# Turning the gathered tokens of five experts: from TensorE to VectorE, by way of DRAM

## The chip, the core and the metric

The program runs on one core of a Trainium2 chip. A core has five engines that run their own queues of instructions and wait for one another by semaphores: TensorE (PE, matrix products; its weight loads are shown as PEld), VectorE (DVE), ScalarE (ACT), GpSimd (POOL) and SyncE (SP, which here issues most DMAs). SBUF and PSUM are memories of 128 partitions; PE writes to PSUM alone. The metric is device time in microseconds of one execution, the median of several runs.

## The reference

Three layers follow one another on B x S = 2304 tokens of 512 values: attention that keeps the 32 largest scores of each row, a gated layer, and a layer with eight experts of which each token uses one. The change is in the third:

```python
def _moe2_ref(x, expert_emb, tau, w1, w2):
    xn = x / (np.linalg.norm(x, axis=-1, keepdims=True) + 1e-06)
    en = expert_emb / (np.linalg.norm(expert_emb, axis=-1, keepdims=True) + 1e-06)
    logits = xn @ en.T / tau
    expert_idx = np.argmax(logits, axis=1)
    ...
    for e in range(E):
        mask = expert_idx == e
        ...
        h = np.maximum(x[mask] @ w1[e], 0.0)
        out[mask] = gate_w[mask, None] * (h @ w2[e])
```

## The kernel before, in words

Attention and most of the gated layer fill the first 768 us, ordered by lists of names that are written out by hand. They leave the gated layer's result in DRAM (`y_dram`, one row of 512 values for each token), and a table in DRAM (`tbl`) that lists the tokens of each expert. What follows is the expert layer, again with an order written by hand (`tc.manual_schedule()`): each engine runs its instructions in the order of the code.

The experts are sorted by their number of tokens. Rank r has room for `CAPS[r]` tokens, (480, 352, 320, 304, 256, 256, 256, 240), cut into blocks of 128: 4 + 3 + 3 + 3 + 2 + 2 + 2 + 2 = 21 blocks. "Expert r" below is the expert of rank r. The order of work is `TURNS` = 0, 1, 2, 3, 4, 6, 7, 5; the main loop (line 1225) goes over r, with `then`, the next expert, and `nn`, the one after it.

All products are made of three: a number is split into a high part (rounded to the fp32r format) and the low rest, and high x high, low x high and high x low are added. For one expert r the loop does this:

- **The f loop** (lines 1229 to 1240). For each of eight blocks of 128 hidden columns, `first` (line 961) makes 12 products on PE (line 953, into a PSUM tile of the pool "ph", which has two buffers); ACT writes `hh`, the high part of the clipped result (line 958), and DVE `hl`, the low part (line 959).
- Between the blocks, work for the next expert is put in. `turn_in` (line 1036), after blocks 2, 4 and 6, takes one block of 128 gathered tokens (`xg`), which has a token on each partition, and turns it so that the features are on the partitions: four PE transposes of 128x128 into a PSUM tile `pxt` of the pool "px" (line 1044, two buffers), then ACT writes the high part `xh_` (line 1045) and DVE the low part `xl_` (line 1046). `split_2`, after the odd blocks, splits a quarter of the next expert's second weights: ACT writes `h` (line 860), DVE `l` (line 861).
- Experts 2 and 3 (`ACROSS`) make their second product transposed, and it is turned back in the next expert's f loop by `turn_out` (line 1003) after blocks 0, 2 and 4, with four PE transposes into `pxo`, in the same pool "px"; `leave` then sends the rows to the output with a DMA on POOL (line 1027) and starts the gather of a gate (line 1013).
- **After the f loop** SP issues the four loads of the second weights of `nn` (`load2`, line 857), which wait until the split of `then`'s second weights has read their buffer, and POOL the gathers of `nn`'s tokens (`get`, line 1033) from `y_dram`.
- Then the second product (`second`, line 987, or `columns`, line 1000). After its first block the four pieces of `then`'s first weights are split (`split_1`), and SP issues the loads of `nn`'s first weights (`load1`, line 848).

The features of a token are numbered on the partitions by blocks of 128: partition p of slice k holds feature 128k + p, as `w1r` (line 777) and the slices `xg[:, 128k : 128k+128]` in `turn_in` have it. Elsewhere in the kernel there is another form: `route`, in the gated layer, writes a tile to `yq_dram` and loads it back in another order, so that a transpose of 32x32 squares on DVE (line 685) completes the turn; partition p of slice k then holds feature 4p + k. The last two tiles of that layer are turned by PE with slices of step four (line 1166).

Of the kernel before, what the change touches and what calls it, by code (L numbers as in the profile page):

```python
# [8 lines left out]
F32 = mybir.dt.float32  # L9
# [20 lines left out]

TURNS = (0, 1, 2, 3, 4, 6, 7, 5)
ACROSS = (2, 3)
TURNED = 12
NEG = -3.0e38
BIG = 2.0 ** 100
# [25 lines left out]
def fused_kernel(tc: tile.TileContext, *args):  # L61

    nc = tc.nc
    y_dram = tc.dram_tile([NT + 1, DM], F32, name="y_dram")
    g_dram = tc.dram_tile([NT + 128, 1], F32, name="g_dram")
    tbl = tc.dram_tile([E * STRIDE, 2], I32, name="tbl")

    yq_dram = tc.dram_tile([8, 128, 128], F32, name="yq_dram")  # L70
    lo_dram = [tc.dram_tile([8, 128, 1024], F32, name=f"lo_dram{n}") for n in range(2)]
    with ExitStack() as held:
        pools = [held.enter_context(tc.tile_pool(name=n, bufs=b, **kw)) for n, b, kw in
                 (("const", 1, {}), ("sm", 4, {}), ("fs", 1, {}), ("ps_a", 1, {"space": PSUM}))]
        flag = pools[0].tile([1, 2], I32, name="flag")
        consts = {}
        over_ = layers(tc, *args, y_dram, yq_dram, g_dram, tbl, lo_dram, flag, pools, consts)
        rare = nc.values_load(flag[0:1, 1:2], min_val=0, max_val=NT + 1)  # L78
        with tc.If(rare > 0):
            over_()  # L80
            again = nc.values_load(flag[0:1, 0:1], min_val=0, max_val=1)
            with tc.If(again > 0):
                layers(tc, *args, y_dram, yq_dram, g_dram, tbl, lo_dram, None, pools, consts)()


class Held:
# [7 lines left out]
        return self.tiles[name]  # L94


def layers(tc: tile.TileContext, qt, kt, v, w_in, w_out, embt, tau, w1, w2, out, y_dram, yq_dram, g_dram, tbl, lo_dram, flag, pools, consts):
    nc = tc.nc
    exact = flag is None

# [3 lines left out]
    ident, ent = both[:, 4 * E:], both[:, :4 * E].rearrange("p (k e) -> p k e", k=4)  # L104
# [33 lines left out]
    def bank():  # L138
        turn[1] ^= 1
        return bank_t[turn[1]]  # L140
# [66 lines left out]
    for q in range(8):  # L207
        c = slice(256 * q, 256 * q + 256)
# [368 lines left out]
    moe = deque()  # L577
# [196 lines left out]
    late = {}  # L774
    mb = ExitStack()
    evs, idts, tok, ws1 = {}, {}, {}, {}
    w1r = w1.rearrange("e (k p) f -> p e k f", p=128)

    def blocks(r):
        return [(o // 128, o, min(128, CAPS[r] - o)) for o in range(0, CAPS[r], 128)]  # L780
# [63 lines left out]
    def load1(r, parts=range(4)):  # L844
        if 0 in parts:
            ws1[r] = raw1[r] = late["w1" if r == 0 else "wb"].tile([128, 4, F2], F32, tag="raw", name="a1")
        for k in parts:
            nc.sync.dma_start(out=raw1[r][:, k, :], in_=w1r[:, bass.ds(evs[r], 1), k, :].rearrange("p o f -> p (o f)"))
# [4 lines left out]
    def load2(r, parts=range(4)):  # L853
        if 0 in parts:
            ws2[r] = raw2[r] = late["w1"].tile([128, 8, DM], F32, tag="raw", name="a2")
        for k in parts:
            nc.sync.dma_start(out=raw2[r][:, 2 * k:2 * k + 2, :], in_=w2r[:, bass.ds(evs[r], 1), 2 * k:2 * k + 2, :].rearrange("p o k d -> p (o k) d"))
# [67 lines left out]
    if True:  # L925
# [15 lines left out]
        hs, xg_, gg_, xt_ = {}, {}, {}, {}  # L941
# [19 lines left out]
        def first(r, f, c0, c1):  # L961
            hidden(r, f, c0, c1)
            hidden_out(r, f, c0, c1)
# [66 lines left out]
        def get(r, b):  # L1030
            n, o, m = b
            xg_[r, n] = xg = late["xg"].tile([128, DM], F32, tag="xg", name="xg")
            nc.gpsimd.indirect_dma_start(out=xg[:m, :], out_offset=None, in_=y_dram,
                                         in_offset=bass.IndirectOffsetOnAxis(ap=idts[r][:m, n, 0:1], axis=0))

        def turn_in(r, b):
            n, o, m = b
            if r not in tok:
                tok[r] = [(tk if TURNS.index(r) % 2 else late["tk"]).tile([128, 4, CAPS[TURNS.index(r) % 2]], F32R, tag=t, name=t) for t in ("xh_", "xl_")]
            xh_, xl_ = tok[r]  # L1040
            xg = xg_.pop((r, n))
            pp = bank().rearrange("p (k n) -> p k n", k=4) if moe else px.tile([128, 4, 128], F32, tag="px", name="pxt")
            for k in range(4):
                nc.tensor.transpose(pp[:, k, :m], xg[:m, 128 * k:128 * k + 128], ident[:m, :m])
            nc.scalar.copy(xh_[:, :, o:o + m], pp[:, :, :m])
            nc.vector.tensor_tensor(xl_[:, :, o:o + m], pp[:, :, :m], xh_[:, :, o:o + m].bitcast(F32), op=ALU.subtract)

# [41 lines left out]
        bl = {r: blocks(r) for r in range(E)}  # L1089
# [43 lines left out]
        with tc.manual_schedule():  # L1133
            at.close()
            pools_()
            for n in range(len(moe)):
                a = moe[0]
# [18 lines left out]
            px = mb.enter_context(tc.tile_pool(name="px", bufs=2, space=PSUM))  # L1156
# [57 lines left out]
            todo = [(r, b) for r in TURNS for b in bl[r]]  # L1214
# [10 lines left out]
            for r, then, nn in zip(TURNS, TURNS[1:] + (None,), TURNS[2:] + (None, None)):  # L1225
                c0 = 256 if r == 0 else 0
                b2 = bl[r][2:] if r == 0 else bl[r]
                todo = deque(bl[then]) if then is not None else deque()
                for f in range(8):
                    first(r, f, c0, CAPS[r])  # L1230
                    if back and f in (0, 2, 4):
                        turn_out(*back[0])
                        leave(*back.popleft())
                    if todo and f in (2, 4, 6):
                        turn_in(then, todo.popleft())
                    if then is not None and f % 2:
                        split_2(then, f // 2)
                    if r == 0 and f > 5:
                        leave(0, bl[0][f - 6])
                    if r == 1 and f in (0, 3, 6):  # L1240
                        finish_counts(f // 3)
                if nn is not None:
                    load2(nn)
                    for x in bl[nn]:
                        get(nn, x)
                for n, b in enumerate(b2 if r not in ACROSS else range(4)):
                    if r in ACROSS:
                        columns(r, n)
                    elif n == len(b2) - 1 and then is None:
                        last_block(r, b)  # L1250
                    else:
                        second(r, b, range(8))
                    if n == 0 and then is not None:
                        for k in range(4):
                            split_1(then, k)
                        if nn is not None:
                            load1(nn)
                    if r not in ACROSS:
                        leave(r, b)
                if r in ACROSS:  # L1260
                    back.extend((r, b) for b in b2)
                if nn is None and then is not None:
                    nc.gpsimd.drain()  # L1263
# [93 lines left out]
```

## Time and profile before

| | us |
|---|---|
| median of 3 runs | 1019.8 (1019.55 to 1022.65) |
| profiled execution, its own time | 1016.89 |
| its span, first to last instruction | 1015.1 |
| PE busy | 940.5 (93% of the span) |
| DVE busy | 769.4 (76%) |
| ACT busy | 714.1 (70%) |
| POOL busy | 631.7 (62%) |
[...]

The profile is of one execution. In a row of busy time by stretch stand the stretch, its length, then the busy time of PE, PEld, DVE, ACT and POOL with the number of instructions, PE's granted clock, the DMA engines' busy share and GB/s. Busy time of PE is that of overlapping records: products are pipelined, so the time that one costs is the distance from its start to the next start. In the timelines the columns are start, duration, engine, line, operation, what is written and read, and in brackets the idle time of the engine before it with what ended it.

### The profile page before, as it was taken

To read this page: it belongs to the slowest core of one execution; us is meant where nothing else is said; L and a number is where in the kernel's file an instruction comes from. 1 tells how busy PE (TensorE), PEld (TensorE's weight loads), DVE (VectorE), ACT (ScalarE), POOL (GpSimd) and SP (SyncE) were. 2 spreads that over 40 slices of the span, in tenths; PEclk is the share of its full clock that TensorE was granted. 3 is DMA by queue.
4 is the path that set the end of the run, shared out by engine and by line. 5 is a ranking of instruction groups with operands and counts; after the bars stand their busy time and mean duration, and the time that the engine had idled before them with its cause. 6 is when DMAs were issued, how large, how long until landed. Compare 5 with 4: busy or idle time off the path is not lost. (4 is left out here: it accounts for less than half of the span.)

```text
span 1015.1 us, 20760 instructions
## 1 busy us (share of the span) xinstructions
PE 940.5 (93%) x7172; PEld 825.0 (81%) x7172; DVE 769.4 (76%) x2353; ACT 714.1 (70%) x1441; POOL 631.7 (62%) x786
## 2 busy tenths in 40 slices
PE   3666787999999999999999999999999999999997
PEld 1344576889899988998999987889898888999996
DVE  7999999999989989889999898871234464455551
ACT  4899898888789788798787787774335553455551
POOL 4788999877778788688687775674242353034220
PEclk9965799999999999999999999999999999999999
DMA  5555777664456755556565485375585475545620
GB/s 199 180 166 172 236 242 260 216 206 148 141 175 192 238 183 140 153 166 211 195 183 147 141 256 191 123 235 187 170 280 195 134 245 202 185 153 194 235 83 23
DMA packets 93265, 187.25 MB, mean 184 GB/s; under 512 B 15837, under 2 KB 36464, under 8 KB 93151
## 3 DMA queue, kind: packets, MB, share of 16 engines
q1 hardware_dynamic: 88591, 175.97, 54.2%
q0 software_dynamic: 4416, 9.80, 3.0%
q8 instruction: 58, 0.95, 0.4%
q14 instruction: 56, 0.46, 0.1%
q10 hardware_dynamic: 144, 0.07, 0.0%
HBM read 160.56 MB, written 22.03 MB: 180 GB/s over the span
## 5 line engine op out<-in xcount | busy, mean ns | idle before, releaser
L490 POOL TENSOR_TENSOR s<-s,z 128x576 f32<-128x576 f32 x144 | 189.8, 1319 | 62.1 <-ACT z L486 61.6
L605 PE MATMUL bank_h<-xh,vh 128*128 128x256 f32 x576 | 170.8, 297 | 0.0
L605 PE MATMUL bank_h<-xh,lo 128*128 128x256 f32 x576 | 163.2, 283 | 0.7 <-DMA lo<-lo_dram 0.7
L605 PE MATMUL bank_h<-xl,vh 128*128 128x256 f32 x576 | 163.0, 283 | 0.0
L472 DVE MAX8 A<-left 128x8 f32<-128x288 f32 (+1 forms) x288 | 159.4, 594 | 0.0
L523 PE MATMUL bank_t<-both,s 128*128 128x128 f32 x648 | 107.8, 290 | 29.5 <-ACT pt L528 17.3
L523 PEld LDWEIGHTS bank_t<-both,s 128*128 128x128 f32 x648 | 81.3, 148 | 51.7 <-ACT pt L528 22.8
L528 ACT COPY pt<-bank_t 128x384 f32<-128x384 f32 x216 | 101.5, 479 | 26.4 <-PE bank_t L523 26.4
L624 POOL TENSOR_TENSOR gl<-u,gh 128x512 fp32r<-128x512 f32 x72 | 93.2, 1294 | 42.4 <-ACT gh L621 42.3
L444 ACT COPY s<-ps_sc 128x576 f32<-128x576 f32 x143 | 92.3, 645 | 36.0 <-PE ps_sc L433 13.3
L640 PE MATMUL y<-wh,gh 128*128 128x512 f32 x288 | 116.8, 406 | 0.0
L486 ACT ACTIVATE z<-s,nb 128x576 bf16<-128x576 f32 x144 | 112.3, 780 | 4.7 <-POOL nb L480 4.5
L640 PE MATMUL y<-lo,gh 128*128 128x512 f32 x288 | 113.5, 394 | 0.1
L640 PE MATMUL y<-wh,gl 128*128 128x512 f32 x288 | 113.3, 393 | 0.0
L496 ACT ACTIVATE s<-s,nb 128x576 f32<-128x576 f32 x144 | 113.0, 786 | 0.2 <-POOL s L490 0.2
L605 PEld LDWEIGHTS bank_h<-xh,lo 128*128 128x128 f32 x576 | 110.1, 191 | 0.9 <-DMA lo<-lo_dram 0.9
L605 PEld LDWEIGHTS bank_h<-xl,vh 128*128 128x128 f32 x576 | 110.5, 192 | 0.3
L605 PEld LDWEIGHTS bank_h<-xh,vh 128*128 128x128 f32 x576 | 110.4, 192 | 0.3
L1027 POOL DMA_INDIRECT out_dram<-ob,idt x21 | 23.1, 1100 | 135.2 <-ACT ob L1020 108.5
L541 PE MATMUL bank_a<-pt,vt 128*64 128x128 f32 (+1 forms) x1600 | 94.9, 278 | 0.6 <-ACT pt L528 0.6
L959 DVE SCALAR_TENSOR_TENSOR hl<-ph,hh 128x256 fp32r<-128x256 f32 (+5 forms) x72 | 31.7, 440 | 84.1 <-ACT hh L958 83.7
L861 DVE TENSOR_TENSOR l<-a,h 128x1024 fp32r<-128x1024 f32 x64 | 76.8, 1234 | 24.2 <-ACT h L860 23.6
(263 smaller groups left out, 2636.2 us busy)
## 6 DMA issues: line engine op xcount, KB each, us to landing
lo<-lo_dram SPq DMA_DIRECT2D x144, 512.0 KB, 4.5
a<-in_moe_w_dram SPq DMA_DIRECT2D x64, 512.0 KB, 6.3
vt<-in_v_dram SPq DMA_DIRECT2D x28, 320.0 KB, 5.1
w<-in_moe_w_in_dram SPq DMA_DIRECT2D x16, 512.0 KB, 4.5
w<-in_moe_w_out_dram SPq DMA_DIRECT2D x16, 512.0 KB, 5.5
lo_dram<-wf SPq DMA_DIRECT2D x32, 256.0 KB, 2.4
qraw<-in_q_dram SPq DMA_DIRECT2D x48, 128.0 KB, 3.9
krs<-in_k_dram SPq DMA_DIRECT2D x16, 288.0 KB, 4.2
```

What stands on the lines that cost most here:

```text
L444: nc.scalar.copy(sbuf[i % NS][:, :, HS * g:HS * g + HS], ps_[i][:, :, :HS])
L472: nc.vector.max(A[:, n, 8 * r:8 * r + 8], src[:, n, :w])
L486: nc.scalar.activation(zb_[n], tile_of(i, n), AF.Relu, bias=sel[i][1][:, n, 1:2], scale=-BIG)
L490: nc.gpsimd.tensor_tensor(s, s, zb_[n], op=ALU.subtract)
L496: nc.scalar.activation(s, s, AF.Exp, bias=sel[i][1][:, n, 0:1], scale=SCALE, accum_out=sums[i][:, n:n + 1])
L523: nc.tensor.transpose(pp[:, 128 * k:128 * k + 128], e[:, 128 * (3 * c + k):128 * (3 * c + k) + 128], ident)
L528: nc.scalar.copy(pts[i][:, 3 * c:3 * c + 3, :].rearrange("p k n -> p (k n)"), tb_.pop((i, c))[:, :384])
L541: nc.tensor.matmul(av[64 * n:64 * n + 64, c0:c1], vt[:, k, 64 * n:64 * n + 64], pt[:, k + 5 * n if k < 4 else 4, c0:c1], start=(o == 0), s ...
L605: nc.tensor.matmul(ph[:, a, :], w, x[:, k, :], start=(k == 0 and n == 0), stop=(k == 3 and n == 2))
L624: nc.gpsimd.tensor_tensor(state[q][1], state.pop((q, "u")).rearrange("p (a n) -> p a n", a=2), state[q][0].bitcast(F32), op=ALU.subtract)
L640: nc.tensor.matmul(state["y"][o], x[:, a, c], w, start=(f == 0 and n == 0), stop=(f == 15 and n == 2))
L861: nc.vector.tensor_tensor(lo, x, hi.bitcast(F32), op=ALU.subtract)
```

## The change

Five of the eight experts (`CARRIED` = 3, 4, 5, 6, 7; all but the first three of the order of work) have their tokens turned by DVE in place of PE. As soon as their rows are gathered, SP stores them to a DRAM tile `xq_dram` (`carry_out`), ahead of the loads of the second weights. After the first block of the second product it loads them back in another order (`carry_in`), ahead of the loads of the first weights: partition 32a + c then holds 128 features (those of group a) of tokens 4c to 4c + 3. In the next f loop DVE transposes the 32x32 squares into `pxt` (`turn_x`, after blocks 1, 3 and 5), and `turn_in` goes on from there without its PE transposes. The gathers of these experts always bring 128 rows, since whole tiles are stored. As the result has feature 4p + k on partition p of slice k, the first weights are loaded in that order for all experts, and the PE transposes that stay (experts 0, 1, 2) take slices of step four.

```diff
-    w1r = w1.rearrange("e (k p) f -> p e k f", p=128)
+    w1r = w1.rearrange("e (p k) f -> p e k f", k=4)
...
             xg_[r, n] = xg = late["xg"].tile([128, DM], F32, tag="xg", name="xg")
+            if r in CARRIED:
+                m = 128
...
+        def carry_out(r):
+            for n, o, m in bl[r]:
+                nc.sync.dma_start(out=xq_dram[n].rearrange("a p x -> p a x"), in_=xg_[r, n].rearrange("p (a x) -> p a x", a=4))
+
+        def carry_in(r):
+            for n, o, m in bl[r]:
+                nc.sync.dma_start(out=xg_[r, n], in_=xq_dram[n].rearrange("a (c i) x -> (a c) (i x)", i=4))
+
+        turned_ = {}
+
+        def turn_x(r, b):
+            n, o, m = b
+            turned_[r, n] = pp = px.tile([128, 4, 128], F32, tag="px", name="pxt")
+            nc.vector.transpose(pp.rearrange("p k (c i) -> p i k c", i=4), xg_[r, n].rearrange("p (i r k) -> p i k r", i=4, k=4))
...
-            pp = bank().rearrange("p (k n) -> p k n", k=4) if moe else px.tile([128, 4, 128], F32, tag="px", name="pxt")
-            for k in range(4):
-                nc.tensor.transpose(pp[:, k, :m], xg[:m, 128 * k:128 * k + 128], ident[:m, :m])
+            if r in CARRIED:
+                pp = turned_.pop((r, n))
+            else:
+                pp = bank().rearrange("p (k n) -> p k n", k=4) if moe else px.tile([128, 4, 128], F32, tag="px", name="pxt")
+                for k in range(4):
+                    nc.tensor.transpose(pp[:, k, :m], xg[:m, :].rearrange("p (x k) -> p k x", k=4)[:, k], ident[:m, :m])
...
                     first(r, f, c0, CAPS[r])
+                    if todo and f in (1, 3, 5) and then in CARRIED:
+                        turn_x(then, todo[0])
...
                 if nn is not None:
-                    load2(nn)
                     for x in bl[nn]:
                         get(nn, x)
+                    if nn in CARRIED:
+                        carry_out(nn)
+                    load2(nn)
...
                         if nn is not None:
+                            if nn in CARRIED:
+                                carry_in(nn)
                             load1(nn)
```

How the instructions stand: first DVE in expert 6's f loop, from `hl` of block 1 on. Before (`hl` and `hh` are the parts of the first product of block ph, `a`, `h` and `l` the second weights of expert 7 and their parts, `xh__` and `xl__` its tokens' parts):

```order
1316 L959 SCALAR_TENSOR_TENSOR hl_11812<-ph2_11828,hh_11811 128x256
1317 L861 TENSOR_TENSOR l2_11844<-a2_11723,h2_11843 128x1024
1318 L959 SCALAR_TENSOR_TENSOR hl_11812<-ph2_11847,hh_11811 128x256
1319 L1046 TENSOR_TENSOR xl__11863<-pxt_11864,xh__11862 128x4x128
1320 L959 SCALAR_TENSOR_TENSOR hl_11812<-ph2_11871,hh_11811 128x256
1321 L861 TENSOR_TENSOR l2_11844<-a2_11723,h2_11843 128x1024
1322 L959 SCALAR_TENSOR_TENSOR hl_11812<-ph2_11888,hh_11811 128x256
1323 L1046 TENSOR_TENSOR xl__11863<-pxt_11903,xh__11862 128x4x112
```

The same place of DVE with the change:

```order
1323 L961 SCALAR_TENSOR_TENSOR hl_11810<-ph2_11826,hh_11809 128x256
1324 L1053 STREAM_TRANSPOSE pxt_11841<-xg_11717 128x4x128
1325 L863 TENSOR_TENSOR l2_11844<-a2_11723,h2_11843 128x1024
1326 L961 SCALAR_TENSOR_TENSOR hl_11810<-ph2_11847,hh_11809 128x256
1327 L1068 TENSOR_TENSOR xl__11863<-pxt_11841,xh__11862 128x4x128
1328 L961 SCALAR_TENSOR_TENSOR hl_11810<-ph2_11866,hh_11809 128x256
1329 L1053 STREAM_TRANSPOSE pxt_11881<-xg_11719 128x4x128
1330 L863 TENSOR_TENSOR l2_11844<-a2_11723,h2_11843 128x1024
1331 L961 SCALAR_TENSOR_TENSOR hl_11810<-ph2_11885,hh_11809 128x256
```

A transpose stands between `hl` of each of the blocks 1 and 3 and the split of the second weights behind it. Then SP, around the loads of one expert's second and first weights (rows of register work between the loads are marked ISA). Before:

```order
480 L857 ISA
481 L857 DMA a_11410<-in_moe_w_dram 128x2x512
482 L857 ISA
483 L857 DMA a_11410<-in_moe_w_dram 128x2x512
484 L857 ISA
485 L857 DMA a_11410<-in_moe_w_dram 128x2x512
486 L857 ISA
487 L857 DMA a_11410<-in_moe_w_dram 128x2x512
488 L848 ISA
489 L848 DMA a_11456<-in_moe_w_dram 128x1024
```

The same place of SP with the change:

```order
484 L1042 DMA xq_dram<-xg 128x4x128 x2
485 L859 ISA
486 L859 DMA a_11412<-in_moe_w_dram 128x2x512
487 L859 ISA
488 L859 DMA a_11412<-in_moe_w_dram 128x2x512
489 L859 ISA
490 L859 DMA a_11412<-in_moe_w_dram 128x2x512
491 L859 ISA
492 L859 DMA a_11412<-in_moe_w_dram 128x2x512
493 L1046 DMA xg<-xq_dram 128x512 x2
494 L850 ISA
495 L850 DMA a_11456<-in_moe_w_dram 128x1024
```

The two stores stand ahead of the second weights' loads, the two loads back between them and the first weights' loads.

## Rows read from the trace of the kernel before

**Rows 1.** F loops of experts 2, 3, 4, 6, 7: length, busy time by engine.

```profile
855.66:871.16 15.50, 15.50 (x110) 15.21 (x108) 8.31 (x13) 8.00 (x14) 4.76 (x5) 1.00 0.22 66
885.24:900.87 15.63, 15.63 (x119) 15.60 (x118) 8.11 (x12) 9.22 (x16) 7.36 (x8) 1.00 0.32 113
914.20:927.90 13.70, 13.70 (x118) 13.68 (x118) 7.48 (x12) 8.93 (x16) 6.75 (x7) 1.00 0.38 139
939.05:951.32 12.27, 12.27 (x105) 12.27 (x104) 7.27 (x12) 7.31 (x13) 4.80 (x4) 1.00 0.65 237
962.46:974.22 11.76, 11.76 (x105) 11.73 (x104) 7.06 (x12) 7.28 (x13) 2.45 (x2) 1.00 0.51 204
```

**Rows 2.** Timeline of PE, expert 6: a turn after block 2, and the second product's start.

```profile
943.33 0.60 PE L1044 MATMUL pxt<-both,xg 128*128 128x128 f32 x4
943.69 0.36 PE L953 MATMUL ph<-xh__11614,h 128*128 128x256 f32 x1
943.89 0.28 PE L953 MATMUL ph<-xl__11615,h 128*128 128x256 f32 x1
944.00 0.28 PE L953 MATMUL ph<-xh__11614,l 128*128 128x256 f32 x1
...
951.32 0.39 PE L987 MATMUL po<-h,hh 128*128 128x512 f32 x1
```

**Rows 3.** Timeline of PE: a turn with slices of step four.

```profile
769.79 0.65 PE L1166 MATMUL pxt<-both,ysl 128*128 128x128 f32 x4
770.20 0.36 PE L953 MATMUL ph<-xh__9917,h 128*128 128x256 f32 x1
```

**Rows 4.** Line 685, ns min/median/max of one, first and last start.

```profile
L685 DVE STREAM_TRANSPOSE yt<-ya x12: 1078/1100/1129, 240.4 to 614.2; 128x512 f32<-128x512 f32 x12
```

**Rows 5.** Groups by line on DVE: busy us, mean ns of one, idle before.

```profile
L454 DVE TENSOR_TENSOR left<-ps_sc,s 128x288 f32<-128x288 f32 x72 | 32.9, 457 | 2.5
L453 DVE TENSOR_TENSOR ps_sc<-ps_sc,s 128x288 f32<-128x288 f32 x72 | 32.8, 456 | 12.7 <-ACT s L444 12.2
```

**Rows 6.** Timeline of DVE in expert 6's f loop, blocks 1 and 2.

```profile
942.52 0.42 DVE L959 SCALAR_TENSOR_TENSOR hl<-ph,hh 128x256 fp32r<-128x256 f32 x1 [1.00 <-ACT hh L958]
943.45 1.22 DVE L861 TENSOR_TENSOR l<-a,h 128x1024 fp32r<-128x1024 f32 x1 [0.51 <-ACT h L860]
944.60 0.42 DVE L959 SCALAR_TENSOR_TENSOR hl<-ph,hh 128x256 fp32r<-128x256 f32 x1
944.93 0.68 DVE L1046 TENSOR_TENSOR xl__11863<-pxt,xh__11862 128x512 fp32r<-128x512 f32 x1
```

**Rows 7.** Timeline of DVE in expert 1's f loop.

```profile
833.90 0.50 DVE L959 SCALAR_TENSOR_TENSOR hl<-ph,hh 128x352 fp32r<-128x352 f32 x1
```

**Rows 8.** Timeline of PE at the same place.

```profile
834.46 0.43 PE L953 MATMUL ph<-xh__10431,h 128*128 128x352 f32 x1 [0.44 <-DVE hl L959]
```

**Rows 9.** Timeline of POOL after expert 4's f loop: the last gather.

```profile
928.97 0.94 POOL L1033 DMA_INDIRECT xg<-y_dram,idt  x1 [0.30 <-issue]
```

**Rows 10.** DMA issues from 800 to 1005 us: count, KB, median us to landing.

```profile
a<-in_moe_w_dram SPq DMA_DIRECT2D x48, 512.0 KB, 6.5
...
xg<-y_dram,idt POOLq DMA_INDIRECT x14, 3.4
```

**Rows 11.** Timeline of SP: expert 7's second weights, then its first.

```profile
930.72 2.09 SPq L857 DMA_DIRECT2D a<-in_moe_w_dram  x4
935.26 1.94 SPq L848 DMA_DIRECT2D a<-in_moe_w_dram  x4
```

**Rows 12.** Timeline of ACT in expert 6's f loop: the first split.

```profile
942.38 1.04 ACT L860 CAST h<-a 128x1024 fp32r<-128x1024 f32 x1
```

**Rows 13.** Line 674, the store in pieces of 512 bytes (512 KB).

```profile
L674 SPq DMA_DIRECT2D yq_dram<-ysb x6: 462/466/470, 217.2 to 582.3; - x6
...
DMA to landing us min/median/max: 4.7/4.7/4.8
```

**Rows 14.** Line 678, the load back in pieces of 2 KB (512 KB).

```profile
DMA to landing us min/median/max: 5.2/6.0/6.3
```

More of the change, by code (lines that the diff above doesn't have):

```diff
@@ L32 @@
 ACROSS = (2, 3)
+CARRIED = (3, 4, 5, 6, 7)
 TURNED = 12
@@ L70, in fused_kernel @@
     yq_dram = tc.dram_tile([8, 128, 128], F32, name="yq_dram")
+    xq_dram = tc.dram_tile([3, 4, 128, 128], F32, name="xq_dram")
     lo_dram = [tc.dram_tile([8, 128, 1024], F32, name=f"lo_dram{n}") for n in range(2)]
@@ L76, in fused_kernel @@
         consts = {}
-        over_ = layers(tc, *args, y_dram, yq_dram, g_dram, tbl, lo_dram, flag, pools, consts)
+        over_ = layers(tc, *args, y_dram, yq_dram, g_dram, tbl, xq_dram, lo_dram, flag, pools, consts)
         rare = nc.values_load(flag[0:1, 1:2], min_val=0, max_val=NT + 1)
@@ L82, in fused_kernel @@
             with tc.If(again > 0):
-                layers(tc, *args, y_dram, yq_dram, g_dram, tbl, lo_dram, None, pools, consts)()
+                layers(tc, *args, y_dram, yq_dram, g_dram, tbl, xq_dram, lo_dram, None, pools, consts)()
 class Held:
@@ L94, in tile, with layers @@
         return self.tiles[name]
-def layers(tc: tile.TileContext, qt, kt, v, w_in, w_out, embt, tau, w1, w2, out, y_dram, yq_dram, g_dram, tbl, lo_dram, flag, pools, consts):
+def layers(tc: tile.TileContext, qt, kt, v, w_in, w_out, embt, tau, w1, w2, out, y_dram, yq_dram, g_dram, tbl, xq_dram, lo_dram, flag, pools, consts):
     nc = tc.nc
```

## The prediction

> **What bounds the kernel now.** I read the page first (PE is busy for 93% of the span, and in the last ten slices the other engines are far below that), then the busy time by stage, then PE's own order of time. The change touches only the last stage, the second expert layer, which runs from about 768 us to the end. [rows 1] cuts out the loop over eight column blocks ("the f loop", lines 1229 to 1240) of the five experts during which a changed turn is done: 2, 3, 4, 6 and 7, in the order of work, which turn in the tokens of experts 3, 4, 6, 7 and 5. [...] So PE sets the end here, and every microsecond taken off PE comes off the time, unless another engine holds PE up. That DVE is at half load says less than it seems: PE has two PSUM buffers for the first product (the pool "ph"), so block f+2 can't start before DVE has written `hl` of block f.
>
> **What is removed.** Four PE transposes for each of 11 blocks of tokens (3 blocks for expert 3, two each for 4, 6, 7, 5). What one group costs is its slot on PE, not the 0.27 us of one record, since the records overlap. In [rows 2] the group of expert 7's first block starts at 943.33, the next product at 943.69, and that product's successor 0.20 us later, where 0.11 or 0.12 is usual: 0.36 + 0.08 = 0.44 us. A group that follows a turn_out pays the refill anyway (0.36), and one of 48 rows less. Two whole and one short block (1.1), 2 x 0.36 in each of two loops (1.4), 0.44 + 0.40, and 2 x 0.44: about 4.3 us. That is the most that the change can give.
>
> **What the remaining PE turns pay.** Because the weights' rows are now taken in steps of four, the ten groups of experts 0, 1 and 2 read their tokens with a step of 16 bytes. Such groups exist: line 1166 takes 0.41 us from its start to the next product [rows 3], 0.05 more than [rows 2]. The capacities make 21 blocks; 11 lose their group, 10 keep it: 10 x 0.05 = +0.5 us.
>
> **What DVE gets.** One STREAM_TRANSPOSE of 128x512 for each block, in program order between `hl` of block 1, 3 or 5 and the split of the second weights. The kernel has this instruction already: 1.10 us, 1.08 to 1.13 over 12 runs [rows 4], from SBUF into SBUF, reading with a step of 16 bytes and writing without one. The new one reads with the same step, and writes into PSUM with a step of 16 bytes. That the destination is PSUM costs nothing in the nearest rows: the same 128x288 operation takes 456 ns into PSUM and 457 ns into SBUF [rows 5]. No row has a stepped write of DVE. I take 1.10; the lower bound is 0.69, what DVE takes to stream the same 512 columns out of PSUM [rows 6], the upper 2.2, if each stepped write takes twice as long as a plain one.
>
> [...]
>
> **Where DVE's time lies.** Not beside idle time. I walk expert 6's loop with starts from [rows 6]. There `hl` of block 1 starts at 942.52, the split at 943.45, the next `hl` at 944.60 (1.15 after the split), `xl` at 944.93 (0.33 after), for 0.68. The only gap is the 0.58 us after 942.87, when DVE is free and the split still waits for ACT. After the change: the turn at 942.87, the split 1.03 later at 943.90 (an instruction behind another starts some 0.07 before that one's end), `hl` of block 2 at 945.05, done at 945.47. PE, without its transposes, is through with block 3 at 943.33 + 1.42 ((12.27 - 0.84) / 8 from rows 1) = 944.75 and waits for that `hl`. Expert 1's loop has such a wait: `hl` starts at 833.90 and runs 0.50 us [rows 7], and PE starts at 834.46 [rows 8], 0.06 us after its end, to which I add the 0.08 us of refill from rows 2. So block 4 starts in effect at 945.6, 0.85 us late. `xl` at 945.38, `hl` 3 at 945.98, the second turn at 946.33, the split at 947.36, `hl` 4 from 948.51 to 948.93; block 5 ends at 948.45, and block 6 waits until 949.1. Two more blocks give 951.9, where the trace has 951.32 [rows 2]: **+0.6 us in place of -0.85**.
>
> The others go by the same walk. From `hl` 1 to `hl` 3 a pair of blocks with a turn takes DVE 945.98 - 942.52 = 3.46 us, some 0.1 more where there are more columns. PE's block is the length in [rows 1] less its turns, over eight. Expert 2: (15.50 - 1.15) / 8 = 1.79, a pair 3.58, so DVE keeps up but for a little of its first delay: -0.95 of the 1.15. Expert 3: a pair of 3.39 and 0.43 for a turn_out, so nothing is lost: -0.7. Expert 4: 2.87 + 0.43 = 3.3, nearly enough: -0.15. Expert 7: 2 x 1.36 = 2.72, as expert 6 (2.84): +0.6. The five loops: -0.95 - 0.7 - 0.15 + 0.6 + 0.6 = **-0.6 us**. This moves by some 0.9 us for each 0.1 us that the turn is longer than 1.10; for a turn of 0.8 us it would be -2.7.
>
> **The way by DRAM.** SP issues everything in order. The store waits for the gathers, and behind it stand the four loads of the second weights. In five turns of the loop I compared the gathers with the load's old start. The worst is expert 4's: the last gather starts at 928.97 [rows 9] and lands 3.4 us later [rows 10], at 932.4; the second weights were issued from 930.72 on [rows 11]. With two stores ahead (0.47 us each) they go from 933.3 on, 2.6 us later; a load takes 6.5 us to land [rows 10], so the first is there at 939.8, and ACT wants it at 942.38 [rows 12]: hidden. The load back waits for the store, 4.7 us for twice the bytes in pieces of the same 512 bytes [rows 13], so 937.3 at the latest, and takes 5.2 to 6.3 us [rows 14]: 942.5 to 943.6, wanted at 942.87. The first weights, behind it, move from 935.26 [rows 11] to about 938.5; they are wanted when the f loop is over, after 951.32: hidden. In the other four loops the block is back 2 us or more ahead. I take +0.3 us for expert 7's turn (0 to +0.8). Nothing waits for the wider gathers of the two short blocks (128 rows each) or for the added traffic; the first weights' reads keep their pieces of 4 KB and only take them at every fourth row, and even the late ones above land at 938.5 + 1.5 + 6.5 = 946.5, 5 us before they are wanted, so 0.
>
> **Sum:** -0.6 + 0.5 + 0.3 = +0.2 us. The profiled execution took 1016.89 us, of which 1015.1 are its span, 2.9 less than the median, 1019.8. The sum of differences holds for either; on the median it gives **1020.0 us**.
>
> **Rivals.** (1) The stepped write is dear, and DVE becomes the bound of all five loops. It decides from a turn of about 1.4 us, where the loops cost some 0.9 x 3 - 0.6 = +2.1 and the sum nears +3; at 1.6 us the sum is +5, about 1025, and at 2.2 us +10, about 1030. For it: the step of 16 bytes on the write is in no row; against it: reads with the same step already run at 1.10. [...]
> (2) The turn is nearly free: at 0.7 us the loops give some -3, the sum -2.2 (1017.6), and with the full 4.3 less 0.5, 1016. For it, that PE is never waiting in rows 1; against, the 1.08 us that is the least of rows 4.
> (3) The blocks come back late in every loop, not in one: a turn that waits stands ahead of the split and of `hl`, so PE stops for nearly as long. One microsecond in each of five loops is +5: 1025. It decides from 0.6 us in each. Against it are the margins above; for it, that DMA load is high in expert 6's loop (0.65 in rows 1).
>
> **Chances.** The wash, -2 to +2.5 us: 0.65. Rival 1: 0.13, rival 2: 0.10, rival 3: 0.12. Under 0.3% (3.06 us) is about what a measurement of this kernel can't tell from no change. Faster: half of rival 2 and a sliver of the wash, 0.07. Slower: most of 1 and 3 and a sliver, 0.22. The same: 0.71. The range, 1017.0 to 1024.5, takes in the wash with the milder halves of the rivals.
>
> **What would show it.** STREAM_TRANSPOSE into "pxt" near 1.1 us, 11 of them; PE idle in front of "ph", released by DVE's `hl`, some 0.8 us twice each in the loops of experts 6 and 7, little in 2 and 3; expert 6's loop about 12.9 us and not 12.27, expert 2's about 14.55 and not 15.5. Wrong would be a turn above 1.4 us, a DVE that waits for the DMA of "xg" in several loops, or PE without waits and a gain near 4 us.

## The result and the profile after

| | before | after |
|---|---|---|
| median, us (runs beside each other) | 1018.7 | 1025.6 |
| ratio, 95% interval | | 1.0064 [1.0051, 1.0077] |
| profiled execution, us (its span) | 1016.9 (1015.1) | 1027.5 (1025.4) |
| bytes moved by DMA, MB | 187.3 | 193.2 |

The change costs 7 us, where +0.2 was forecast, and the time lies above the range. The profiled executions differ by 10.6 us; how much of that is the change's is read loop by loop. The busy time by stage for the f loops of experts 2, 3, 4, 6 and 7 in the changed kernel (stretch, its length, busy time of PE, PEld, DVE, ACT and POOL with instructions, granted clock, DMA share, GB/s), to be laid beside [rows 1]:

```profile
858.15:872.57 14.42, 14.34 (x98) 14.05 (x97) 10.51 (x15) 7.73 (x14) 5.52 (x6) 1.00 0.51 172
886.54:901.30 14.76, 14.76 (x110) 14.72 (x109) 9.76 (x14) 9.21 (x16) 7.20 (x7) 1.00 0.37 134
914.74:927.97 13.23, 13.10 (x110) 12.81 (x109) 9.22 (x14) 8.92 (x16) 5.09 (x5) 1.00 0.54 210
939.11:960.84 21.73, 14.31 (x98) 14.10 (x96) 9.46 (x14) 7.11 (x13) 4.58 (x4) 0.76 0.80 284
971.97:984.33 12.36, 11.30 (x97) 10.91 (x96) 9.07 (x14) 7.16 (x13) 2.33 (x2) 1.00 0.66 261
```

Four of the five loops came out near the forecast: -1.1, -0.9, -0.4 and +0.6 us (expert 4's stretch in [rows 1] starts 0.1 us ahead of its first product; from there on it was 13.61 us). Expert 6's loop, in which expert 7's blocks are turned, went from 12.27 to 21.73 us. It is the only one with a granted clock under 1.00, and the only one in which PE's busy time (14.31) is far from the length. The second products behind these five loops kept their lengths to 0.1 us. PE's timeline in that loop (start, length, line, operands, and in brackets the idle time before it and who ended it):

```profile
944.57 0.28 PE L955 MATMUL ph<-xl__11617,h 128*128 128x256 f32 x1
944.69 0.28 PE L955 MATMUL ph<-xh__11616,l 128*128 128x256 f32 x1
952.39 0.58 PE L955 MATMUL ph<-xh__11616,h 128*128 128x256 f32 x1 [7.42 <-DVE hl L961]
952.77 0.42 PE L955 MATMUL ph<-xl__11617,h 128*128 128x256 f32 x1
952.99 0.41 PE L955 MATMUL ph<-xh__11616,l 128*128 128x256 f32 x1
```

PE stands still for 7.42 us and then steps by 0.22 us where it stepped by 0.12. DVE's timeline at the same place says why `hl` was late:

```profile
942.57 0.42 DVE L961 SCALAR_TENSOR_TENSOR hl<-ph,hh 128x256 fp32r<-128x256 f32 x1 [1.00 <-issue]
949.81 1.09 DVE L1053 STREAM_TRANSPOSE pxt<-xg 128x512 f32<-128x512 f32 x1 [6.81 <-DMA xg<-xq_dram]
950.81 1.20 DVE L863 TENSOR_TENSOR l<-a,h 128x1024 fp32r<-128x1024 f32 x1
951.93 0.40 DVE L961 SCALAR_TENSOR_TENSOR hl<-ph,hh 128x256 fp32r<-128x256 f32 x1
```

The transpose stands first in DVE's order and waits 6.81 us for the load back of expert 7's first block; the split and `hl` of block 2, which need nothing of it, stand behind it. By line 1053 alone (ns min/median/max of one), this is the only one of 11 transposes that waited for its data, and it runs as long as the one in [rows 4]:

```profile
L1053 DVE STREAM_TRANSPOSE pxt<-xg x11: 1089/1115/1140, 862.8 to 979.0; 128x512 f32<-128x512 f32 x11
...
  DMA xg<-xq_dram: 6.8, 1
```

SP's timeline (issues; line 1042 is the store, 859 the second weights, 1046 the load back, 850 the first weights) shows where the block was:

```profile
933.94 4.34 SPq L1042 DMA_DIRECT2D xq_dram<-xg  x2
938.47 2.09 SPq L859 DMA_DIRECT2D a<-in_moe_w_dram  x4
940.66 1.25 SPq L1046 DMA_DIRECT2D xg<-xq_dram  x2
942.10 3.35 SPq L850 DMA_DIRECT2D a<-in_moe_w_dram  x4
```

The second store leaves at the end of its row, near 937.9, since only then has the second gather landed. The second weights go 7.7 us later than in [rows 11], and the load back, right behind these four loads (2 MB) in the same queue, is issued at 940.7 and used at 949.81: 9.1 us. After the stop PE runs on slowly, as the windows of that loop show (same columns as above, the granted clock third from the end):

```profile
939.11:944.80 5.69, 5.69 (x49) 5.65 (x47) 0.85 (x2) 2.78 (x5) 2.92 (x3) 1.00 0.91 273
944.80:952.10 7.30, 0.17 (x2) 0.00 (x0) 2.29 (x3) 1.17 (x3) 0.93 (x1) 0.73 1.04 406
952.10:958.00 5.90, 5.61 (x26) 5.61 (x27) 4.34 (x7) 1.53 (x4) 0.73 (x1) 0.50 0.66 245
958.00:960.84 2.84, 2.84 (x25) 2.84 (x24) 1.98 (x3) 1.62 (x3) 0.00 (x0) 0.94 0.27 76
```

Before the wait the granted clock is 1.00; from 952.1 to 958.0 it is 0.50, and over the last 2.84 us of the loop 0.94.

### The profile page after: what moved, and what is told of

Same layout as the page of the kernel before. It is cut to its first block, busy times and chain, and to the rows that moved or that the text cites. A ratio compares the mean times of both kernels' runs of the same rounds, so it can differ in the third digit from the quotient of the medians.

```text
span 1025.4 us, 20707 instructions
## 1 busy us (share of the span) xinstructions
PE 941.4 (92%) x7128; PEld 825.3 (80%) x7128; DVE 781.2 (76%) x2364; ACT 713.0 (70%) x1441; POOL 631.8 (62%) x786
## 5 line engine op out<-in xcount | busy, mean ns | idle before, releaser
L514 POOL TENSOR_SCALAR s<-s,sums 128x576 f32<-128x576 f32 x112 | 82.4, 747 | 19.9 <-DVE sums L505 19.4
```

The costliest lines, as they stand in the source:

```text
L514: nc.gpsimd.tensor_scalar(x, x, rv[:, n:n + 1], 1.0, op0=ALU.mult, op1=ALU.mult)
```

## The experiments

Theory A: one load back that comes late, with the slow clock behind it, is the whole loss. Theory B: VectorE's turns cost something in every loop. Theory C: the new order of rows in w1 and PE's turns in steps of four cost it. Each run is set against runs of the kernel before on the same chip (medians 1017.8 us for the first four runs below, 1017.4 for the order turned round and for the last two, 1018.5 for the other four).

**One expert back to PE.**

```diff
-CARRIED = (3, 4, 5, 6, 7)
+CARRIED = (3, 4, 5, 6)
```

> Expert 7's two blocks are turned by PE again, those of experts 3, 4, 5 and 6 stay with VectorE by way of DRAM. Theory A (one load back, expert 7's, comes late and PE's standing still and slow clock behind it are the whole loss): expert 6's loop goes from 21.7 us back to about 12.3 us, PE waits nowhere over 1 us, and the kernel is about 9 us faster than the changed one: 1016 to 1018 us, 1 us under the kernel before (-1.05, -0.87 and -0.38 in the loops of experts 2, 3 and 4, +0.6 in that of 7, +0.6 for the stepped turns of 12 blocks). Theory B (VectorE's turns cost something in every loop, a fifth of the loss each): about 1.4 us faster than the changed kernel, 1024 us. Theory C (the new order of rows in w1 and PE's turns in steps of four cost it): no faster than the changed kernel, 1025 us or more.

Measured: 1016.4 us, ratio to before 0.998 [0.997, 0.999]; expert 6's loop 12.40 us. Theory A holds and B falls: with four experts still turned by VectorE the kernel is faster than before, and of the changed kernel's loss nothing is left.

**No way by DRAM.**

```diff
-                    if nn in CARRIED:
-                        carry_out(nn)
...
-                            if nn in CARRIED:
-                                carry_in(nn)
```

> The way by DRAM is left out: VectorE turns the gathered rows as they lie, so what the last five experts compute is of mixed-up rows; the number and shape of all other work is the changed kernel's. Theory A: no load back, nothing late, 1017.5 to 1018.7 us, expert 6's loop at 12.9 us (before 12.27 and 0.6 for VectorE). Theory B: still 1024 to 1025 us. Theory C: 1025 us.

Measured: 1015.8 us, ratio 0.9966 [0.9953, 0.9978], 2 us better than the forecast of theory A. Expert 6's loop takes 12.72 us, with all transposes in place, and those of 2, 3, 4 and 7 are those of the changed kernel to 0.04 us. So the loss is in the way by DRAM, and the walk of DVE against PE came out near the forecast. Most of the 2 us does not stand in these loops. In the two profiles 1.5 us stand in the first f loop of expert 0 (it has two, this one for its first 256 tokens: 17.16 us before, 15.70 here), which varies between profiles for no reason found (last section).

**No turn on VectorE, but the new order of rows.**

```diff
-CARRIED = (3, 4, 5, 6, 7)
+CARRIED = ()
```

> No block is carried or turned by VectorE; PE turns all 21 blocks of the experts in steps of four from w1's new order of rows. Theory A: the kernel before and 21 times 0.05 us, 1019.2 to 1020.2 us. Theory B: the same, 1019 to 1020 us, since no turn is VectorE's. Theory C: the loss of the changed kernel or more, 1025 us and over, spread over all loops.

Measured: 1018.5 us, ratio 1.0005 [0.9996, 1.0015]. Theory C falls. The seven f loops with a turn in them grow by 0.06 to 0.36 us each, 1.2 us in all in the two profiles; the times can't tell it from nothing.

**The whole way issued earlier for expert 7.**

```diff
+                    if nn == 7 and f == 4:
+                        for x in bl[nn]:
+                            get(nn, x)
+                        carry_out(nn)
+                        carry_in(nn)
```

> Expert 7's two gathers, its store and its load back are issued inside expert 4's f loop (after f = 4), ahead of its second weights; nothing else differs from the changed kernel. Theory A (the block came late for where it was issued): both blocks are back before expert 6's loop starts, that loop falls from 21.7 to about 12.9 us, the kernel to 1017 to 1019 us. If the lateness sits in the transfers themselves (store and load of 256 KB each that are slow wherever they stand), PE still waits several us in expert 6's loop and the time stays over 1022 us. Theory B: no change, 1025 us.

Measured: 1020.8 us, ratio 1.0025 [1.0012, 1.0037]; expert 6's loop 15.85 us. This lies between the two expectations. The block was on time and something else was late. SP's timeline in this run:

```profile
933.11 3.68 SPq L1042 DMA_DIRECT2D xq_dram<-xg  x2
937.11 2.13 SPq L1046 DMA_DIRECT2D xg<-xq_dram  x2
939.49 2.53 SPq L859 DMA_DIRECT2D a<-in_moe_w_dram  x4
```

DVE's timeline, the first transpose:

```profile
942.00 1.09 DVE L1053 STREAM_TRANSPOSE pxt<-xg 128x512 f32<-128x512 f32 x1
```

ACT's timeline, the first cast of the second weights:

```profile
944.04 1.04 ACT L862 CAST h<-a 128x1024 fp32r<-128x1024 f32 x1 [2.41 <-DMA a<-in_moe_w_dram]
```

With nothing ahead of them the two loads back land 2.7 us after their issue, and the transpose starts straight behind `hl`. But now SP stands in front of the store and the load back while the second weights wait behind them, and ACT waits 2.41 us for these, PE behind it 2.67 us. The gathers themselves had hardly moved: in GpSimd's order they stand behind three row stores, and started at 929.2 and 931.0.

**The order turned round, for expert 7: second weights first.**

```diff
+                    if nn == 7:
+                        load2(nn)
                     if nn in CARRIED:
                         carry_out(nn)
-                    load2(nn)
+                    if nn != 7:
+                        load2(nn)
```

> For expert 7 alone the order on SyncE is turned round: its second weights' four loads are issued ahead of its store, as in the kernel before, and its load back follows the store directly; gathers and everything else are the changed kernel's. If the 2 MB ahead of the load back are what made it late: the loads are issued near 929 us, the second store near 938, the load back near 938.5 with the queue empty ahead of it, and lands 2.6 to 5 us later, by 941 to 943.5 us; PE waits under 1 us in expert 6's loop (12.7 to 13.5 us) and the kernel takes 1016 to 1018 us. If the late gathers decide by themselves, or the transfer is slow in any place: PE still waits 3 us or more, loop over 16 us, 1020 us and more.

Measured: 1020.5 us, ratio 1.0026 [1.0009, 1.0043]; PE waits 2.96 us and expert 6's loop takes 15.92 us. SP's timeline:

```profile
933.20 2.31 SPq L859 DMA_DIRECT2D a<-in_moe_w_dram  x4
935.61 3.77 SPq L1042 DMA_DIRECT2D xq_dram<-xg  x2
945.18 1.14 SPq L1046 DMA_DIRECT2D xg<-xq_dram  x2
```

DVE's timeline, the first transpose:

```profile
947.77 1.09 DVE L1053 STREAM_TRANSPOSE pxt<-xg 128x512 f32<-128x512 f32 x1 [2.36 <-DMA xg<-xq_dram]
```

The load back, with the queue empty ahead of it, is there 2.6 us after its issue, not 9.1. But the store pays instead: the second one leaves near 939, and SP can issue the load back only at 945.18, some 6 us later. So the 2 MB in front cost whichever of the two transfers stood behind them: the load back 9.1 us in the changed kernel, the store some 6 us here. My expectation that the store would land as fast as in an empty queue was the miss here.

**The load back on another queue.**

```diff
+                if nn == 7:
+                    for n, o, m in bl[nn]:
+                        nc.gpsimd.dma_start(out=xg_[nn, n], in_=xq_dram[n].rearrange("a (c i) x -> (a c) (i x)", i=4))
```

> Expert 7's load back alone moves from SyncE's queue, where it stood behind the four loads of second weights, to GpSimd's queue, at the end of expert 4's second products; its gathers and its store stay where they were. Theory A1 (the load back waited its turn behind the 2 MB in its own queue): it lands some 5 us after its store, near 946 to 947 us rather than 949.8, PE waits about 4 us rather than 7.4, and the kernel takes 1020 to 1022 us. Theory A2 (the transfers share the engines, the queue does not matter): it lands at 949 us or later as before, 1025 us. Theory A3 (the late gathers alone decide): the same time as A2's.

Measured: 1025.3 us, ratio 1.006 [1.004, 1.0081]; expert 6's loop 22.06 us. POOL's timeline, the issue:

```profile
940.87 1.22 POOL L1290 DMA_DIRECT2D xg<-xq_dram  x2
```

DVE's timeline, the transpose that waits:

```profile
947.90 1.09 DVE L1053 STREAM_TRANSPOSE pxt<-xg 128x512 f32<-128x512 f32 x1 [7.19 <-DMA xg<-xq_dram]
```

From its own queue the load takes 7.0 us and not 9.1, while 4 MB of weights are under way (DMA share 0.98 from 940.87 to 947.90). It was issued 4.1 us into the loop (after: 1.6 us), so nothing is gained in the end, and the time is the one that theories A2 and A3 forecast. The three durations suggest that most of the 7 us against 2.6 is the share of the engines and that some 2 us are the place in the queue, so A1 was too simple; this split is argued, not shown, since no run gives the load the other queue without the weights beside it.

**The clock by itself.**

```diff
+                    if r == 6 and f == 3:
+                        fill = po_.tile([128, DM], F32, tag="po", name="fill")
+                        for _ in range(62):
+                            nc.tensor.matmul(fill[:, :256], ws1[r][0][:, 0, 0:128], tok[r][0][:, 0, 0:256], start=True, stop=True)
```

> Added work, whose result nothing reads: after the products of f = 3 in expert 6's loop PE makes 62 more matmuls of 128x256 (about 7.2 us at full clock) in the stretch in which it stood waiting; all else is the changed kernel. If the slow clock behind the wait costs by itself (about 2.6 us by the trace: 6 us at half speed), the granted clock stays at 1.00 through 944 to 960 us, expert 6's loop falls from 21.7 to about 19 us and the kernel to about 1023 us. If the clock's fall costs nothing because the weights of the split are late anyway, the loop stays at 21.7 us and the kernel at 1025.6 us.

Measured: 1023.8 us, ratio 1.0046 [1.003, 1.0063]. Expert 6's loop takes 19.51 us. Its windows:

```profile
937.91:944.80 6.89, 6.89 (x59) 6.89 (x58) 0.85 (x2) 2.80 (x5) 2.92 (x3) 1.00 0.96 288
944.80:952.00 7.20, 7.20 (x61) 7.07 (x60) 3.50 (x6) 1.81 (x3) 1.66 (x1) 1.00 1.04 407
952.00:957.42 5.42, 5.17 (x43) 4.97 (x43) 4.86 (x8) 2.52 (x5) 0.00 (x0) 1.00 0.68 237
```

PE works through the stretch in which it stood, the granted clock stays at 1.00, and the loop is 2.2 us shorter although PE does 62 matmuls more. DVE waits for the load back as before (6.71 us). So of the loop's 9.5 us 2.2 are the slow clock's, 6.8 the wait, and 0.5 what VectorE's turns cost with a block on time (12.72 against 12.27). The medians are too close to show the 2.2 us: 1.0046 and 1.0064, with intervals that overlap.

**The gathers and the store earlier, for experts 6, 7 and 5.**

```diff
                 for f in range(8):
+                    if nn in (6, 7, 5) and f == 2:
+                        for x in bl[nn]:
+                            get(nn, x)
+                        carry_out(nn)
                     first(r, f, c0, CAPS[r])
```

> The gathers and the store of experts 6, 7 and 5 are issued at f = 2 of the f loop before, ahead of GpSimd's waits for the rows out; the loads back stay behind the second weights. Theory A: gathers land by 928 us, stores go out before the second weights are due, no block is late and the second weights are not either; expert 6's loop 12.7 to 12.9 us, the kernel like the one without the way by DRAM, 1015.5 to 1017.5 us. If a load back behind 2 MB is late by itself, even with an early gather, PE still waits over 2 us in expert 6's loop and the time stays over 1019 us.

Measured: 1017.0 us, ratio 0.9977 [0.9963, 0.9991]; expert 6's loop 12.74 us. SP around the same place:

```profile
923.69 1.78 SPq L1042 DMA_DIRECT2D xq_dram<-xg  x2
929.96 2.09 SPq L859 DMA_DIRECT2D a<-in_moe_w_dram  x4
932.14 0.90 SPq L1046 DMA_DIRECT2D xg<-xq_dram  x2
934.50 2.10 SPq L850 DMA_DIRECT2D a<-in_moe_w_dram  x4
```

The gathers start at 919.6 and 921.6, ahead of two of the three row stores that GpSimd waits for, the stores are issued 4 us before the second weights, and these go 8.3 us ahead of the loop, as in [rows 11]. The load back still stands behind 2 MB, but now from 932.1 on, 6 us before the loop begins: it takes 8.4 us to land and is in time. So the late gather is what all the other lateness hung on: with it every order on SP that was tried loses, without it the order of the change does no harm.

**The turns moved into the second products.** On top of still earlier gathers, stores and loads back, `turn_x` and `turn_in` of experts 6, 7 and 5 follow the split of the first weights:

```diff
                             load1(nn)
+                        if nn in (6, 7, 5):
+                            for x in bl[nn]:
+                                turn_x(nn, x)
+                                turn_in(nn, x)
```

> As the run before, with the gathers, stores and loads back of experts 6, 7 and 5 still earlier (loads back ahead of the second weights), and the turns and splits of their blocks moved out of the f loop, where VectorE is late, into the second products before it, where it has 6 us to spare. The loops of experts 4, 6 and 7 then hold products alone: 13.2, 11.5 and 11.0 us against 13.61, 12.27 and 11.77 of the kernel before; with the gains of 1.05 and 0.87 in those of 2 and 3 and 0.7 lost to stepped turns 3 to 4 us under the kernel before: 1014 to 1015.5 us. If the blocks are late there, the second products grow or VectorE's first split of the next loop waits, and the time is over 1017 us.

Measured: 1015.4 us, ratio 0.9973 [0.9957, 0.9989]. The f loops of experts 4, 6 and 7 in this run:

```profile
911.07:923.76 12.69, 12.69 (x111) 12.67 (x110) 6.79 (x11) 8.68 (x17) 4.97 (x4) 1.00 0.75 242
934.89:946.70 11.81, 11.63 (x97) 11.43 (x96) 6.75 (x11) 6.80 (x13) 5.43 (x5) 1.00 0.50 197
957.84:971.16 13.32, 11.31 (x98) 10.93 (x96) 8.65 (x13) 7.24 (x14) 3.71 (x4) 1.00 0.91 342
```

Two loops hold almost nothing but products and, in expert 4's, the turns back of expert 3's result; in expert 7's, PE waits 1.73 us for a first `hl`, after expert 5's load back had come 2.38 us late for its transpose; expert 5's gathers stood behind a row store for which GpSimd waits 4.46 us. The next run takes that away, and the stepped turns with it:

```diff
+                    if r == 4 and n == 0:
+                        for x in bl[5]:
+                            get(5, x)
...
-                    nc.tensor.transpose(pp[:, k, :m], xg[:m, :].rearrange("p (x k) -> p k x", k=4)[:, k], ident[:m, :m])
+                    nc.tensor.transpose(pp[:, k, :m], xg[:m, 128 * k:128 * k + 128], ident[:m, :m])
```

(with w1 loaded in its old order for experts 0, 1 and 2)

> The second-product version once more, with expert 5's gathers issued in expert 4's second products, ahead of a row store that GpSimd waits 4.5 us for, and with the old order of rows in w1 and PE's plain turns for experts 0, 1 and 2. If the 1.7 us wait in expert 7's loop came of expert 5's late load back, that loop falls from 13.3 to 11.2 us; with 0.5 us for the plain turns the time is 1012.5 to 1014 us, 4.5 to 6 us under the kernel before. If the wait has another cause (the splits moved beside the second products), loop 7 stays at 13 us and the time at 1015 us.

Measured: 1015.5 us, ratio 0.998 [0.9962, 0.9998]. Expert 7's loop fell to 11.32 us as expected, but expert 6's rose to 12.66 in its profile (PE waits 0.18 and 0.40 us for `hl` there; why stays open), and the time is that of the run before it, not 1013. The two can't be told apart; by their intervals both are faster than the kernel before, and so than the changed one. From the end of that first f loop of expert 0 to the end of the program, their profiles are 0.9 and 2.0 us shorter than that of the kernel before, where the medians give 3.1 and 2.0; the rest of the 3.1 may be that loop again (15.70 us in both).

**Control: PE turns in those same places.**

```diff
-CARRIED = (3, 4, 5, 6, 7)
+CARRIED = ()
...
                             for x in bl[nn]:
-                                turn_x(nn, x)
                                 turn_in(nn, x)
```

> A control: the gathers of experts 6, 7 and 5 and the turns and splits of their blocks stand where they stand in the run before this one, but PE turns all blocks, nothing goes by DRAM, and w1 keeps its old order. If the gain comes of taking PE's turns away, PE spends the same 0.4 us for each block in another place and the kernel takes 1017.5 to 1019.5 us, as the kernel before. If it comes of the new places (VectorE relieved in the f loops), 1013 to 1016 us.

Measured: 1018.4 us, ratio 1.0002 [0.9986, 1.0018]. Expert 4's second product, then expert 6's f loop, in this run:

```profile
927.65:939.62 11.97, 11.97 (x58) 9.81 (x57) 7.63 (x9) 6.72 (x9) 2.97 (x4) 1.00 0.63 218
939.62:951.43 11.81, 11.66 (x97) 11.44 (x96) 6.10 (x10) 6.19 (x11) 2.97 (x3) 1.00 0.56 223
```

The f loop is as short as with VectorE's turns, and the second product is 0.83 us longer than the 11.14 us that it takes without turns: 0.42 us for each of two blocks, paid in another place. So the gain of the two versions above is PE's turns taken away, as the prediction priced them, and not the new places: this control and the run before it, on the same chip, are 3.0 us apart, where the prediction put the eleven groups at 4.3 us at most.

## Why the prediction was wrong

**Right: what bounds, and what the turns are worth.** PE sets the end in [rows 1], where its busy time is the length of each of the five stretches at a granted clock of 1.00. The slot of 0.44 us for a group is what the control shows in another place (0.42). The transpose takes 1.115 us, against 1.100 in [rows 4], so rival 1 falls: the write into PSUM in steps of 16 bytes costs 0.015 us here. The doubling behind its upper end, 2.2 us for a turn, was the author's assumption, and no run shows it: the longest of the 11 turns took 1.140 us. Rival 2 falls by the same times.

**Right in kind, near in size: the walk of DVE against PE.** Forecast -0.95, -0.7, -0.15, +0.6 (experts 2, 3, 4, 7), measured -1.1, -0.9, -0.4, +0.6. For expert 6 it forecast a loop of 12.27 + 0.6 us; with a block on time it is 12.72 and 12.74. There PE waits twice for `hl`, as forecast, but for less than the 0.8 us each that the prediction looked for (with earlier gathers):

```profile
944.71 0.39 PE L955 MATMUL ph<-xh__11622,h 128*128 128x256 f32 x1 [0.55 <-DVE hl L961]
948.07 0.39 PE L955 MATMUL ph<-xh__11622,h 128*128 128x256 f32 x1 [0.24 <-DVE hl L961]
```

The stepped turns: 0.05 us forecast for each group; in the run without a turn on VectorE the seven f loops grow by 1.2 us for 17 groups, 0.07 each.

**Wrong: one term, the way by DRAM in expert 7's turn.** It was put at +0.3 us (0 to +0.8), and the loop shows 9.46 - 0.6 = some 9 us. Step by step, with times of that chain (the landing of the gather is taken from the issue of the second store):

| step | as forecast | as traced |
|---|---|---|
| last gather starts | 928.97 | 931.88 |
| it has landed | 932.4 | 937.9 |
| second weights issued | 933.3 | 938.5 |
| load back issued | 937.3 | 940.7 |
| load back landed | 942.5 to 943.6 | 949.8 |

Three things were taken from rows that didn't hold there. The gather's start was the old one. In the changed kernel POOL's second row store of expert 4's loop is held back, and the gathers behind it:

```profile
919.09 0.97 POOL L1015 DMA_INDIRECT gg<-g_dram,idt  x1 [0.30 <-issue]
923.27 1.01 POOL L1029 DMA_INDIRECT out_dram<-ob,idt  x1 [3.21 <-ACT h L862]
926.83 1.74 POOL L1029 DMA_INDIRECT out_dram<-ob,idt  x1 [1.29 <-ACT h L862]
930.14 1.43 POOL L1037 DMA_INDIRECT xg<-y_dram,idt  x1 [0.30 <-DMA out_dram<-ob,idt]
931.88 1.96 POOL L1037 DMA_INDIRECT xg<-y_dram,idt  x1 [0.31 <-DVE l L863]
```

In the kernel before, the gap ahead of this store is 1.29 us; here it is 3.21. The DMA share next to it, of the changed kernel and then of the one without the way by DRAM (where the gap is 1.29 us and the store starts at 919.91):

```profile
918.00:921.00 3.00, 3.00 (x28) 3.00 (x27) 2.35 (x3) 2.61 (x5) 1.75 (x2) 1.00 0.96 373
921.00:924.00 3.00, 2.87 (x25) 2.64 (x24) 3.00 (x6) 2.18 (x5) 0.73 (x1) 1.00 0.04 14
```

```profile
915.00:918.00 3.00, 3.00 (x28) 3.00 (x26) 1.21 (x3) 2.21 (x4) 1.35 (x2) 1.00 0.48 191
918.00:921.00 3.00, 2.87 (x24) 2.66 (x23) 3.00 (x6) 2.58 (x6) 1.62 (x2) 1.00 0.20 74
```

Expert 6's own store and load back have pushed its second weights 2 us towards its first (both counted from the start of expert 4's loop), the engines are busy until 921, 6 us into that loop and not 3, and the row store goes 2 us after they fall idle. The run without expert 7's turn, which still carries expert 6, holds this store back as well (3.37 us), so expert 7's own way is not what does it. In five runs that hold it back (by 2.88 to 3.37 us) the gather of a gate just ahead of it took 3.2 to 3.7 us to land, the longer the later the store; in three with the gap of 1.29 us it took 2.3 to 2.5. That the store waits for a transfer and not for the ACT instruction that the profile names is argued from this, not shown.

Second, 3.4 us for a gather to land was the median over many [rows 10]; this one took 6.0; why stays open (the engines' share was 0.61 in that time, and 0.64 in that of the old gather). Third, the 5.2 to 6.3 us of [rows 14] are those of loads in another place of the kernel, whatever stood ahead of them there. Behind 2 MB the load back took longer everywhere: 6.9 to 7.8 us in the run without expert 7's turn, where a landing can be read, and no block was late there. The change sets the second weights in front of the load back; the prediction counted what the stores cost the weights, and did not count what the weights cost the load back. That is 3 to 4 of the 6.8 us; the later issue is the other 3.4. The wait then passed through DVE's order to PE, as rival 3 said, but in one loop, where it said every loop, and at 6.8 us, where it said 1. The 2.2 us of slow clock behind it were in no step.

**The sum, made again.** The five loops: -1.1 - 0.9 - 0.4 + 0.6 + 9.5 = +7.7 us. Expert 0's second f loop, expert 1's f loop and the second product behind expert 0's first f loop, where PE's turns are stepped, add 0.7, 0.3 and 0.2 us. Half a microsecond of this is not the steps': with the same turns expert 0's loop grew by 0.2 us in the run without the way by DRAM, and with plain turns by 0.7 us in the last version with turns in the second products. From expert 0's first product to the last second product the profiles differ by 8.8 us in all, and 1.4 us more lie ahead of it. The medians give 7.0 (5.2 to 7.8 by the interval); the profiled execution of the changed kernel is the slowest of its eight, and where the difference to 8.8 lies is not shown.

## What to carry to other kernels

A round trip through DRAM is priced from the last moment at which its data can be fetched and from what is ahead of it in its queue at that moment, not from the duration of a lone transfer (here 9.1 us behind 2 MB, where the same load took 2.6 and 2.7 with its queue empty ahead of it); the tightest of several like loops decides, and there every start in the chain has to be worked out anew. An instruction that waits for such a trip belongs as late in its engine's order as its consumer allows, with work that needs nothing of it in front (this follows from the stopped split and `hl`; no run moves the transpose alone). Before moving a fetch forward on the issuing queue, see whether its own source (here a gather behind row stores on GpSimd) can come earlier: that took away the whole loss here (1017.0 us), while the other orders on the issuing queue left some 2.6 us of it (1020.8 and 1020.5 us).

## What the runs showed of the hardware

- The same load back of 256 KB took 2.6 and 2.7 us with its queue empty ahead of it (order turned round, whole way earlier), 7.0 us from another queue beside 4 MB of weights, and behind 2 MB in its own 9.1 us in the changed kernel and 8.4 us with earlier gathers.
- After 7.4 us in which PE stood still it ran at a granted clock of 0.50 for about 6 us; 2.2 us of the loop were lost to that, and filler matmuls gave them back (one profile each). Behind PE's waits of 2.67 us (whole way earlier) and 2.96 us (order turned round) it ran slowly too: the granted clock was 0.63 from 949 to 952 us in the first and 0.50 from 950.3 to 953.0 in the second.
- The profiled executions of different kernels fall into two groups in a place that the edits touch at most by the order of rows in w1, the first f loop of expert 0: some 17.1 us (before, after, and six others) or 15.7 us (five, the one without expert 7's turn among them), with a granted clock between 777 and 787 us of 0.83 to 0.90 in the first group and of 1.00 in the second. PE's wait of 0.5 us near 776 us stands ahead of both, so what decides it stays open. It is why whole spans of single profiles are not compared here.
- A DVE transpose of 128x512 that writes into PSUM in steps of 16 bytes takes 1.115 us, against 1.100 us for the one into SBUF without such steps.
